# Sinkhorn attention and a bilinear feed-forward on one core: a gate on batch 0's second halves, and q of two more head pairs transposed by DMA

## Chip, core and metric

The kernel runs on one core of one Trainium2 chip. The metric is the time of one execution on the device in microseconds, as a median of several runs; lower is better. TensorE is called PE in the profile (its weight loads PEld), VectorE DVE, ScalarE ACT, GpSimd POOL, SyncE SP.

## What is computed

Four batches, eight heads, 768 tokens, 64 values a head. The sequence is cut into 8 blocks of 96. A small 8 by 8 matrix for each head is normalised five times over rows and columns and mixes the blocks of k and v; attention then runs inside each block. The heads are put side by side (512 values a token) and go through a feed-forward of two projections, their product, and an output projection.

```python
for _ in range(5):
    P = P - max(P, -1); P = exp(P)
    P = P / (sum(P, -1) + 1e-9); P = P / (sum(P, -2) + 1e-9)
k_s = einsum('bhij,bhjcd->bhicd', P, k_blocks)   # the same for v
attn = softmax(q_blocks @ k_s.T / 8)             # 96 x 96 in each block
x = (attn @ v_s) as (4 * 768, 512)
out = ((x @ w_a) * (x @ w_b)) @ w_out            # w_a, w_b 512 x 1536, w_out 1536 x 512
```

Inputs and output are fp32; the kernel's matmuls take bf16, which the loads make of the inputs.

## The kernel before

Heads are worked two at a time: a batch has four pairs, and 128 partitions hold two heads of 64. For a pair the steps are:

- q is transposed (`q_part`): twelve TensorE transposes (`q_pe`, L555) into a PSUM bank and a copy out by ACT or DVE into qT. Where `QDMA(b, p)` holds, which it does for batch 3, there is one DMA transpose on SP instead (`q_dma`, L707), and q is loaded by two DMAs with 64 values to a piece (`q_wide`, L434) instead of one (L483).
- k and v are mixed (`mix_half`, L582, for batch 0; `mix_part`, L571, for the others), and copied out to kT and vT.
- v is brought to tokens by TensorE transposes (`v_pe`, L641), or from the seventh pair on by one mix in token order (L619) and a trip through DRAM on SP (L628 out, L632 back).
- scores (L660), exponential on ACT (L665), output (L675), reciprocal and product on DVE (L681, L686).
- x is transposed: for batch 0 by TensorE (`x_part`, L694) and a copy, for the others by one DMA transpose a pair on SP (L702).

Batch 0 is worked in two halves of four blocks each, h = 0 and h = 1, so that the feed-forward of the first half of its tokens can begin early. Its two projections are plain matmuls (`ab_plain`, L836). Batches 1 to 3 use seven products in place of eight (`ab_strassen`, L930); sums of weights and of x that these need run on DVE or POOL (L373). The output projection is `out_plain` (L987), its results go to DRAM from SP (L1007). Until 32.6 us of the plan, gaps of TensorE are filled with matmuls on zeros (`warm`, L1222).

All loads are issued by POOL, in order. `load` lets about 2.8 MB of loads be on their way at a time.

Nothing is scheduled by hand line by line. Each step is a piece of work (`add`) with its engine or a choice of engines, an estimated time, what it depends on, and the buffers and PSUM banks that it takes and gives back. `Plan.solve` goes through the pieces in an order and gives each an engine and a place; the instructions are emitted by the starts that come out. The order is written out: the string ORDER holds for each piece its number and which of its engines it takes. Dependencies of the plan that carry no data, such as the gate of the second halves, shape the plan and so the order that was written out; on the chip an engine waits for data and buffers.

The gate before the change, for batch 0's second halves (L1169 to L1175):

```python
R0 = 10.0
for p in range(HP):
    st["gate", p] = st["last", p]
for p in range(HP):
    rk = R0 + 5.0 * p
    go = st["gate", p]
    qd = q_part(0, p, 1, rk, go)
```

`st["last", p]` is the last piece of pair p's first half (the DVE product of L686).

Of the kernel before, what the change touches and what calls it, by code (L numbers as in the profile page):

```python
# [36 lines left out]
class Plan:  # L37
# [13 lines left out]
    def add(self, eng, dur, fn, deps=(), get=(), put=(), rank=0.0, lat=None, port=()):  # L51

        alts = dict(eng) if isinstance(eng, (list, tuple)) else {eng: dur}
        op = Op(alts, fn, deps, list(get), list(put), rank, lat, len(self.ops), port)
        for key in op.put:
            self.holders[key] = self.holders.get(key, 0) + 1
        self.ops.append(op)
        return op
# [171 lines left out]

RATE = 365e3
ORDER = (
    b"%z1C$e###%#'#)#+#/#-#1#5$g$i#7#;$k$m#A$o#=$q$s#G#3$u$w#C#M$y%^${#I$}#9#S%`%#%%#Y%'#O#?%)%+"
    b"#`#E%-%/#U#f%1%~%3#[#K%5#l&$%7%9#b#r%;#Q%=#W%?#x%A#h%C&@%E#n#^%G&B%I%K#t%M#d#~%O%Q%S#j$(#z"
    b"%U$.&_#p%W&a%Y$4%b%f#v%d$:%[$$&&%h&H)/&(%j&K%n%l&D&*#|%p&G&2$*&L&-&c$@&4$0%r&O&.)+$6%t&e&P"
    b"&1&g$<$&%v&R&o$B$,&j')&q$2'%$F',&T$8''&k&V'-$L$>&X&m&6&}$H)-'0&Z'#'f&8%x&^'^'h&:'b%|'j$D'a"
    b"&<'d$R$N&s'm'C&>&u'?-j'E&w'n'A'G(($J'p'J($$T'O(+$X'K(&'1'N'Q&y-r'|&|(,'3$P(#*0(/$Z*<$_*@-l"
    b"*>$V$a*2*D*B(>*8*4*F(D$]'S(@*6(J-_*H(P(F*:*T(V$c*J(L-Z(](B*V-c*P(c(R'U*L-e*](i(H*m'W(X-f*N"
    b"(N*X(_*R(T*o(o(e(0-i*u*a(u(Z-](k*Z(2({-a(a,8)%*_(q(4,:*c-v(g(6'Y(w*i(8*e(m+f'](}-p*g+i(s(:"
    b")''5*k(<*q(y)1+n'7*s'9)3)7+q)#'r)=*w';+r'=))-n-1+t't+j'v,4+l)9'x,<,7-t'z+v,>,]-3--)5,`+x,D"  # L240
    b")C,@-0,F-x*})?,C*y+z*{)I);+|+~+))O+%,H)E++)U,J,L,N)[)K+1+#)b)A+-,P+')Q)h,$)G+/,&)n)W+A+3)M"
    b")t,()^+C,*)S)z,e,,+I+5)d,g)Y*$+9)j+7,i)`**.Z+=)p,k,R.^+;)f,T+Y,V)v)l.c+?+M)|)r+[.e+O+b*&.g"
    b"+E)x,m+U/1*,.i+G/3)~,a+K,o-5,c*(+^-7+Q*..k,{-9,q,}+S.m+`,s+W-;._,.,00.+d.a/Y0*00,X/].y,2.o"
    b"0-.{,u.P,w.q-=,y,Z-?-#-A-%/^-'-C.(1E-)/`/5-+-K/7/--M.*/0/9.s.,/b.u/A.w../;-z/C/d/f.0/=/K-O"
    b"/M.}/h-Q-|/#/?.R/%-~02.T-E.$04.<-G-I06/j.&-S.V0>.>080@/E.A/O/l-U.2/G/Q.X/I.B/S-W/x0H0:/z/n"
    b".F.D/p0<0J1H/r/|/t1r/~/v.H1t.41I1v0$.J1L1z.6.L1x1M1|0B25.81~1O0D.N2$0F1U2&1Q.:1W2*2(1[1S26"
    b"202,1^221l1Y2.1`1b282:1h0L2<1j1d1n0N2>0P2B1f0V2D0X0]2@2_0c2H0_2a1q2F2Y2J2g0e0i2N0Z2c2i0o2L"
    b"2e0u0a2m2T0k2[2P2o2V0{2k0q2R2q1%0g4P0w2s4T2]2y3'0m4V2{3#2u3)0s3+4R2}2w3/1+3-4X313K0}0y4Z33"
    b"5#3M3%351'3S114]3F371-3O5%173U3;1#391=3Y3Q3A1)3=3[3C3G3W3?4e4_3j3^1/4g3`5O133z3I6L3f3h3l19"
    b"4a5Q4F151?1;3b6$4c/'0&3d4o6&3|3o5W4q/)5'5Y4H0(5)5S1A4#5[4<4J5|/+5U4L5^5d5~5+5f6(4$5-4(6*4N"  # L250
    b"5/5`4&6,4i/U4*514k574m4,5n5b4>0R594s6.4A425p/W4u534w4B0T646044664.5h55475r3p6N4D485j5t6S5l"
    b"625v6{405;6Q6}3r4:5=7#5?3t7'7%3v687)6V6T7+6:6X7>7-3x6<6_7/6Z6a73716e6]7?79756g7;6u6c776i6k"
    b"7A7C6q6>7E6s6w6m7G6@6o7K7I6y6B7M7h6D7O7c7j7Q6F7p7S7l7r7W7U7v7n7d7^7Y7x7`8*7t7[7z7|5A7f8&80"
    b"5C8(8,7~82848$5E88868.8T8:5G8<8O8V8>5I8]8@8X8_8D8B8c8Z8P8J8F8e8L8s8a8H8y8i8R8v9O8k9;4y5K8m"
    b"8x4{5M8g9'5x8o9Y4}8q6H5z8{9)8}9E6J9,9#9[9-919%9^9`9/9b9d939f9G969Q9I9l979T9h9n:u9U9j9=99:w"
    b"9r:'9K9?9p9W9t:y9A:}9x9M9v;#:{:(9z9~;'9C;79|;%;):$:*:,;-;+:.:0;:;3:4:2;/:6;5:J:8;1::;<;=:<"
    b";A;?:@:>;C:L;E:F:B;[:H;G;I:D;K:O:P;M:T:R;Q;O:V;^:X;W;S;Y:Z:o:];U:_;a;b:a;f;d:e:c;h:q;j:k:g"
    b":m;l<$;n:i;p:t<4;r;v<';t<H;|;~;x<R;z<)<J<T<L<6<W<><N<8<:<P<]<X<<<@<_<Z<B<*<b<D<c<,<F<.<0<e"
    b"<2"
)  # L260
STRASSEN_OUT = ()
QDMA = lambda b, p: b >= 3
VDMA = lambda b, p: 4 * b + p >= 6


@with_exitstack
def kernel(
# [259 lines left out]
    s_ok = {}  # L527
# [77 lines left out]
    def mix_copy(eng, b, p, what, h, tc_order):
        mix, to = buf((what + "m", b, p)), buf((what + "T", b, p))
        i0, n = (0, NB) if h is None else (h * NBH, NBH)
        o0 = 0 if h is None else h * HK
        if tc_order:
            copy(ENG[eng], _ap(to, o0, [[2 * HK, P], [1, n * BLK]]),  # L610
                 _ap(mix, i0 * CG, [[1024, P], [1, n * CG], [P, NCH]]))
        else:
            copy(ENG[eng], _ap(to, o0, [[2 * HK, P], [CG, NCH], [BLK, n], [1, CG]]),
                 _ap(mix, i0 * CG, [[1024, P], [P, NCH], [CG, n], [1, CG]]))
# [86 lines left out]
    def x_dma(b, p):  # L701
        nc.sync.dma_start_transpose(  # L702
            out=_ap(buf(("xT", b)), p * S, [[KA * S, P], [BLK, NB], [1, BLK]]),
            in_=buf(("xp", b, p)).rearrange("q i e d -> q (i e d)"))

    def q_dma(b, p):
        nc.sync.dma_start_transpose(  # L707
# [56 lines left out]
    def v_part(b, p, h, vsrc, rk):  # L764

        pe = add("PE", 0.28 if h is not None else 0.5, lambda: v_pe(b, p, h), [vsrc, o_ident],
                 get=[("bank", ("vp", b, p, h))], put=[("vT", b, p)], rank=rk)
        alts = (("ACT", 0.6), ("DVE", 0.42)) if h is not None else (("ACT", 1.0), ("DVE", 0.69))
        op = add(alts, None, None, [pe, o_pads, first.get(("v", b, p))],
                 get=[("vs", ("vs", b, p))] if h in (0, None) else [],  # L770
                 put=[("vp", b, p, h)], rank=rk)
        first["v", b, p] = op
        op.fn = lambda: v_copy(op.eng, b, p, h)
        return op
# [386 lines left out]
    for p in range(HP):  # L1161
        rk = float(p)
        qd = q_part(0, p, 0, rk)
        kd = mix_half(0, p, "k", 0, rk)
        vd = v_part(0, p, 0, mix_half(0, p, "v", 0, rk + 0.05), rk + 0.1)
        m = so_part(0, p, 0, True, kd, qd, vd, rk + 0.1)
        x_part(0, p, 0, m, rk + 0.15)
        st["last", p] = m
    R0 = 10.0  # L1169
    for p in range(HP):  # L1170
        st["gate", p] = st["last", p]
    for p in range(HP):
        rk = R0 + 5.0 * p
        go = st["gate", p]
        qd = q_part(0, p, 1, rk, go)  # L1175
        kd = mix_half(0, p, "k", 1, rk, go)
        vd = v_part(0, p, 1, mix_half(0, p, "v", 1, rk, go), rk + 1.0)
        m = so_part(0, p, 1, True, kd, qd, vd, rk + 1.0)
        x_part(0, p, 1, m, rk + 2.0)
    for p in range(HP):  # L1180
        load_pair(1, p, -2)
    later_spreads(5)
# [128 lines left out]
```

## Time and profile before

| what | value |
|---|---|
| median of 4 runs | 244.28 us (243.34 to 246.06) |
| the profiled execution | 243.34 us, span 241.6 us |
| granted TensorE clock, mean over the span | 0.998 |
| TensorE busy | 231.9 us, 96% of the span |
| DVE, ACT, POOL busy | 152.4, 115.3, 110.3 us |
| chain that ended last | TensorE 92%; L930 34%, L987 26%, L836 13% |
| first L836, first L987 in the chain | 29.91, 76.59 us |
| DMA | 27.88 MB, mean 115 GB/s |

The span runs from the program's first to its last instruction in the profile; the execution's time has 1.7 us around it. The chain is followed back from the last instruction: at each step to the work that released it, or to the instruction before it on its engine. A step called "issue" is time in which the engine waited for nothing that the profile shows.

### The profile page before, as it was taken

The page shows a single profiled execution, that of the slowest core. Times are in us where ns is not written, and L with a number is a line of the kernel's source. Part 1 is how long each engine was busy: PE and PEld are TensorE (multiplying, and loading weights), DVE is VectorE, ACT ScalarE, POOL GpSimd, SP SyncE. Part 2 cuts the span into 40 slices and gives each one's busy share as a digit, 9 for nine tenths or more (in the row PEclk, how much of TensorE's full clock was granted, in tenths as well). Part 3 has the DMA queues.
Part 4 walks back from the last instruction along what each step waited for, and adds up shares of the span by engine and source line. Part 5 has one row for each costly group of instructions (what it writes and reads, how often), then busy time and mean ns, then how long its engine had stood idle before and what let it go on. Part 6 is the DMA issues. An engine that isn't in the chain of part 4 may idle for free.

```text
span 241.6 us, 5480 instructions
## 1 busy us (share of the span) xinstructions
PE 231.9 (96%) x2196; PEld 132.5 (55%) x2196; DVE 152.4 (63%) x305; ACT 115.3 (48%) x174; POOL 110.3 (46%) x123
## 2 busy tenths in 40 slices
PE   8799799999999999999999999999999999999992
PEld 3367565675656555665554555655654455555440
DVE  6758637785746564678873565887663468877410
ACT  3367624485257443656572633666620166564110
POOL 8779999998300000559995004265240005433000
PEclk9999999999999999999999999999999999999999
DMA  5999999999976769319999699200143461000066
GB/s 68 181 200 159 200 170 176 174 188 198 201 167 141 66 152 204 82 42 98 145 197 116 139 200 226 59 3 1 19 49 65 87 138 39 0 0 3 0 130 130
DMA packets 50104, 27.88 MB, mean 115 GB/s; under 512 B 28832, under 2 KB 47008, under 8 KB 50080
## 3 DMA queue, kind: packets, MB, share of 16 engines
q0 software_dynamic: 24112, 14.16, 43.3%
q1 hardware_dynamic: 25968, 13.38, 28.6%
q8 instruction: 17, 0.28, 0.5%
q14 instruction: 7, 0.06, 0.1%
HBM read 30.29 MB, written 8.26 MB: 160 GB/s over the span
## 4 chain that ended last, share of the span: by engine, by line
PE 92%; DMA 2%; POOL 2%; ACT 1%; issue 1%; DVE 0%; ACTq 0%
PE ps L930 34%; PE ps L987 26%; PE ps L836 13%; PE ps L675 4%; PE ps L660 3%; PE ps L571 2%; DMA q<-in_q_dram 2%; PE ps L582 2%; PE ps L555 2%; PE ps L641 1%; PE ps L619 1%; PE ps L1222 1%; PE ps L694 1%; ACT kT L316 1%; POOL k L439 1%
## 5 line engine op out<-in xcount | busy, mean ns | idle before, releaser
L987 PE MATMUL ps<-w_out_sb,hT 128*128 128x512 bf16 x288 | 67.0, 379 | 0.0
L373 DVE TENSOR_TENSOR f<-f,ps 128x768 f32<-128x768 f32 x54 | 49.8, 951 | 22.3 <-PE ps L930 12.2
L373 POOL TENSOR_TENSOR hT<-f 128x384 bf16<-128x384 f32 x35 | 34.4, 1000 | 50.2 <-DVE f L373 50.1
L936 ACT COPY f<-ps 128x768 f32<-128x768 f32 x54 | 42.2, 800 | 29.8 <-PE ps L930 29.5
L987 PEld LDWEIGHTS <-hT 128*128 128x128 bf16 x288 | 26.8, 98 | 29.4
L665 ACT ACTIVATE eT<-ps 96x768 bf16<-96x768 f32 x32 | 24.9, 811 | 17.3 <-PE ps L660 15.5
L373 DVE TENSOR_TENSOR hT<-a,ps 128x384 bf16<-128x384 bf16 x42 | 22.0, 550 | 15.0 <-PE ps L836 11.0
L930 PE MATMUL ps<-tx,ws_a 128*128 128x384 bf16 x108 | 26.4, 326 | 0.1
L930 PE MATMUL ps<-tx,ws_b 128*128 128x384 bf16 x108 | 26.4, 326 | 0.0
L686 DVE TENSOR_TENSOR xp<-ps,rec 96x512 bf16<-96x512 f32 x32 | 21.6, 683 | 0.7
L930 PEld LDWEIGHTS <-ws_b 128*128 128x128 bf16 x144 | 14.1, 98 | 9.3
L930 PEld LDWEIGHTS <-ws_a 128*128 128x128 bf16 x144 | 13.6, 98 | 9.9 <-ACT f L936 0.5
L836 PE MATMUL ps<-xT,w_b_sb 128*128 128x384 bf16 x96 | 18.8, 326 | 0.0
L373 POOL TENSOR_TENSOR tx<-xT 128x768 bf16<-128x768 bf16 x2 | 3.3, 1631 | 34.0 <-DMA out_dram<-o 34.0
L847 ACT CAST a<-ps 128x768 bf16<-128x768 f32 x12 | 9.3, 800 | 19.0 <-PE ps L836 19.0
L836 PE MATMUL ps<-xT,w_a_sb 128*128 128x384 bf16 x96 | 18.2, 326 | 0.0
L966 ACT CAST a<-ps 128x384 bf16<-128x384 f32 x18 | 8.6, 478 | 18.9 <-PE ps L930 18.9
L930 PE MATMUL ps<-xT,w_a_sb 128*128 128x384 bf16 x72 | 17.6, 326 | 0.0
L930 PE MATMUL ps<-xT,w_b_sb 128*128 128x384 bf16 x72 | 17.6, 326 | 0.0
L316 ACT COPY o<-ps 128x512 f32<-128x512 f32 x15 | 8.6, 589 | 17.0 <-PE ps L987 16.8
L316 ACT CAST kT<-ps 128x768 bf16<-128x768 f32 (+1 forms) x19 | 12.9, 683 | 7.3 <-PE ps L571 6.6
L318 DVE COPY o<-ps 128x512 f32<-128x512 f32 x9 | 6.2, 690 | 14.2 <-PE ps L987 13.8
(95 smaller groups left out, 328.4 us busy)
## 6 DMA issues: line engine op xcount, KB each, us to landing
out_dram<-o SPq DMA_DIRECT2D x48, 128.0 KB, 2.4
k<-in_k_dram POOLq DMA_DIRECT2D x16, 192.0 KB, 6.1
v<-in_v_dram POOLq DMA_DIRECT2D x16, 192.0 KB, 6.3
vd<-vm SPq DMA_DIRECT2D x10, 192.0 KB, 3.1
vs<-vd SPq DMA_DIRECT2D x10, 192.0 KB, 3.2
q<-in_q_dram POOLq DMA_DIRECT2D x16, 96.0 KB, 5.1
w_a_sb<-in_moe_w_a_dram POOLq DMA_DIRECT2D x4, 384.0 KB, 6.1
w_b_sb<-in_moe_w_b_dram POOLq DMA_DIRECT2D x4, 384.0 KB, 6.0
```

The lines of the kernel that those rows point to most:

```text
L316: nc.scalar.copy(out=out, in_=in_)
L373: ENG[eng].tensor_tensor(out=out, in0=in0, in1=in1, op=op)
L660: nc.tensor.matmul(sc[:, e, i * BLK:(i + 1) * BLK], lhsT=kT[e * D:(e + 1) * D, at:at + P], rhs=rhs, start=True, stop=True)
L665: nc.scalar.activation(out=buf(("eT", b, p, h))[:, :, 0:HB], in_=buf(("sc", b, p, h))[0:BLK, :, 0:HB], func=AF.Exp, scale=float(scale))
L675: nc.tensor.matmul(ops_[:, e, i * OW:(i + 1) * OW], lhsT=eT[:, e, i * BLK:i * BLK + P], rhs=vs[:, h * NBH + i, e * OW:(e + 1) * OW], start ...
L686: nc.vector.tensor_tensor(out=_ap(xp, h * NBH * 2 * D, [[NB * 2 * D, BLK], [D, 2], [2 * D, NBH], [1, D]]), in0=_ap(ops_, 2, [[1024, BLK], ...
L836: nc.tensor.matmul(pf[:, u, 0:HW], lhsT=w_sb[:, kc, (m + u) * P:(m + u + 1) * P], rhs=buf(("xT", b))[:, kc, t * HW:(t + 1) * HW], start=(k ...
L847: ea = add("ACT", 0.8, lambda: nc.scalar.copy(out=buf(("a", b, t, m)), in_=buf(("pf", b, t, m, "a"))[:, :, 0:HW]), [ps_["a", 1]], get=[("a ...
L930: nc.tensor.matmul(buf(key)[:, n, 0:HW], lhsT=lf(n, j), rhs=rf(j), start=start and j == 0, stop=j == 1, skip_group_check=not start)
L936: return add("ACT", 0.8, lambda: nc.scalar.copy(out=buf((name, b, g)), in_=buf(kA)[:, :, 0:HW]), [dep], get=[("f", (name, b, g))], rank=rk)
L966: e21 = add("ACT", 0.48, lambda: nc.scalar.copy(out=buf(("c21", b, g))[:, 0, :], in_=buf(kA)[:, 0, 0:HW]), [p4], get=[("a", ("c21", b, g)) ...
L987: nc.tensor.matmul(po, lhsT=hT[:, t * 2 + m // G, m % G, c * P:(c + 1) * P], rhs=w_out_sb[:, m, :], start=(m == 0), stop=(m == KO - 1), sk ...
```

## The change

The gate of every pair's second half becomes the last piece of the last pair's first half. `QDMA` also holds for pairs 2 and 3 of batch 2, so their q is loaded by two DMAs each and transposed by SP. ORDER is another string, written for the plan with these pieces. Three new functions or switches come with it: `mix_first`, which with WHOLE false returns the old `mix_half`; XDMA, which is false for all pairs, so that x of batch 0 goes on by `x_part`; and `x_half_dma`, which is then not called. The limit in `load` is as it was. New lines move the line numbers behind them by up to 33 in the changed kernel.

```diff
 ORDER = (
-    b"%z1C$e###%#'#)#+#/#-#1#5$g$i#7#;$k$m#A$o#=$q$s#G#3$u$w#C#M$y%^${#I$}#9#S%`%#%%#Y%'#O#?%)%+"
+    b"1C$e%z###%#'#)#+#/#-#1#5$g$i#7#;$k$m#A$o#=$q$s#G#3$u$w#C#M$y%^${#I$}#9#S%`%#%%#Y%'#O#?%)%+"
 ...
 STRASSEN_OUT = ()
-QDMA = lambda b, p: b >= 3
+QDMA = lambda b, p: 4 * b + p >= 10
 VDMA = lambda b, p: 4 * b + p >= 6
+XDMA = lambda p: False
+WHOLE = lambda p, what: False
 ...
+    def mix_first(b, p, what, rk):
+
+        if not WHOLE(p, what):
+            return lambda h, r, after=None: mix_half(b, p, what, h, r, after)
 ...
+    def x_half_dma(b, p, h):
+        nc.sync.dma_start_transpose(
+            out=_ap(buf(("xT", b)), p * S + h * HB, [[KA * S, P], [BLK, NBH], [1, BLK]]),
+            in_=buf(("xp", b, p))[:, h * NBH:(h + 1) * NBH].rearrange("q i e d -> q (i e d)"))
 ...
     for p in range(HP):
         rk = float(p)
         qd = q_part(0, p, 0, rk)
-        kd = mix_half(0, p, "k", 0, rk)
-        vd = v_part(0, p, 0, mix_half(0, p, "v", 0, rk + 0.05), rk + 0.1)
+        km = mix_first(0, p, "k", rk)
+        kd = km(0, rk)
+        vm = mix_first(0, p, "v", rk + 0.05)
+        vd = v_part(0, p, 0, vm(0, rk + 0.05), rk + 0.1)
+        st["mix", p] = km, vm
 ...
     R0 = 10.0
     for p in range(HP):
-        st["gate", p] = st["last", p]
+        st["gate", p] = st["last", HP - 1]
     for p in range(HP):
         rk = R0 + 5.0 * p
         go = st["gate", p]
         qd = q_part(0, p, 1, rk, go)
-        kd = mix_half(0, p, "k", 1, rk, go)
-        vd = v_part(0, p, 1, mix_half(0, p, "v", 1, rk, go), rk + 1.0)
+        kd = st["mix", p][0](1, rk, go)
+        vd = v_part(0, p, 1, st["mix", p][1](1, rk, go), rk + 1.0)
         m = so_part(0, p, 1, True, kd, qd, vd, rk + 1.0)
-        x_part(0, p, 1, m, rk + 2.0)
+        if XDMA(p):
+            d = sp_dma(1.3, 0.65, lambda p=p: x_half_dma(0, p, 1), [m, x_home(0)],
+                       put=[("xp", 0, p)], rank=rk + 2.0)
+            xT_done.setdefault((0, 1), []).append(d)
+        else:
+            x_part(0, p, 1, m, rk + 2.0)
```

In the built program TensorE's list has 21 matmuls fewer (24 transposes of q fewer, three warm matmuls more), SP's has two DMA transposes more, and POOL's two load issues more. The two lists agree up to TensorE's first 186 instructions, and then order the same pieces differently: the changed one runs the first halves of all four pairs before the second halves.

More of the change, by code (lines that the diff above doesn't have):

```diff
@@ L232 @@
 ORDER = (
-    b"%z1C$e###%#'#)#+#/#-#1#5$g$i#7#;$k$m#A$o#=$q$s#G#3$u$w#C#M$y%^${#I$}#9#S%`%#%%#Y%'#O#?%)%+"
+    b"1C$e%z###%#'#)#+#/#-#1#5$g$i#7#;$k$m#A$o#=$q$s#G#3$u$w#C#M$y%^${#I$}#9#S%`%#%%#Y%'#O#?%)%+"
     b"#`#E%-%/#U#f%1%~%3#[#K%5#l&$%7%9#b#r%;#Q%=#W%?#x%A#h%C&@%E#n#^%G&B%I%K#t%M#d#~%O%Q%S#j$(#z"
-    b"%U$.&_#p%W&a%Y$4%b%f#v%d$:%[$$&&%h&H)/&(%j&K%n%l&D&*#|%p&G&2$*&L&-&c$@&4$0%r&O&.)+$6%t&e&P"
-    b"&1&g$<$&%v&R&o$B$,&j')&q$2'%$F',&T$8''&k&V'-$L$>&X&m&6&}$H)-'0&Z'#'f&8%x&^'^'h&:'b%|'j$D'a"
@@ L237 @@
[L237 to L254, printed above, removed]
@@ L255 @@
-    b"8x4{5M8g9'5x8o9Y4}8q6H5z8{9)8}9E6J9,9#9[9-919%9^9`9/9b9d939f9G969Q9I9l979T9h9n:u9U9j9=99:w"
-    b"9r:'9K9?9p9W9t:y9A:}9x9M9v;#:{:(9z9~;'9C;79|;%;):$:*:,;-;+:.:0;:;3:4:2;/:6;5:J:8;1::;<;=:<"
+    b"%U$.&_#p%W&a%Y$4%f%b#v%h$:%e$$&*%j%[&,%n&g%m)+%p&D&j&c#|&H&F&f%r$*&k&J%t&o$0%v&m&L$@$6&&&q"
+    b"&O%x)/$<&P$&&)&.%|$B$,&s&1&R$2&u&2&w$8&T&4$F$>&}&V&X$L$H'?'#&6'B(()-'%&8(*&:'G'b''$D(,'J'd"
+    b"$N'1(/'C$R'3'K'F')'f-j'N'+'O$J'i&y'-'Q$T&<&|'j&?&Z'/$X'S'm'^&]'U'5-l'W$P'|'`$Z($'7'~*<'9(&"
+    b"*0$_'n$V(>'Y*>'p$a'](D';*D'r'>*2(J't'v$]*4(P*8(@-_'x(V*H'{(F-Z*L(]$c-]*X(c(L-g*6(B(i-a*Z(R"
@@ new lines @@
+    b"*:-v*J(H(X*N*P(N*T(o-c(_*m*R(u(T*V(e({*o-e(Z*])%(k-i(0*u+f(a)1*_,4(q(2-r*q(g+i(w(4,7*s(m(6"
+    b",a)7(8(}+j,c*w)=(s(:,])')C+l+n(=(y*@,`)I)3+q,q)#)O+v,s+r-t*B))+x+u+Y*F)9,$)U+[,&-x--+b+))5"
+    b"-0+z+++|)[)?+~+E+1-p-5+M-7);+A)b-9+-)E-n+C-;+/+I+G)K)A+3)h*})Q)G)n+O+K*y+U)W,(*{)M)t,*-=)^"
+    b",,,e+%+#)S,g-?)z*a+')Y,i,8*$)d-1,:,k*c)`**-3._)j*e*i-A)p)f*g.a+5*k-C)v,{)l+7,},m,<+=)r+9,>"
+    b",o.c+;.e)|,@)x/1+?.g,B*&/Y-K.2.i/3*,)~-M/[,D*(.4,F/^.k.7,N/`,H.8+^,J,P,L+Q.m*.+`0*+S+d.:,R"
+    b",.,0.Z+W/b0,.].(/d,2,T/f,V.y.o/h,X.{.*02.,-E04.P.q..,Z-G-I06/j-O.0/n-Q.R-S/p08,u.F1F.U-U/l"
@@ new lines @@
+    b",w,y.V-W/x.H/z.s0:.K-#/-.X-%.L.<.u/00<.w-'.N/K-)/5/M/A/7.>/C/r-z.A/9-+/t.B/v/;.}0./#/|/%.D"
+    b"00-|1J/~1M/=0$-~0H1O.$1Q/?1H0>0J1S1U0@1r.&1L1W0B1Y0D1t0F1[1m/E1^1z/G/I1`1|1b/O1h2$/Q1n1j1d"
+    b"2&/S1v1f0L2(0N1p2_1x202a0P1~24222c0V2*2g0X0]2e2,2i0c0_2m2.2k2o0e0i2~3'0Z290o2q2s3)0u0a4T2y"
+    b"273/0k4V2{2u0{0q3$314X1%3+2w0g4P0w351+3-0m2:374Z330s2<3E4R393;4]3%5'3A2B5)3C3G0}0y3=2D5#2>"
+    b"113?1'4_2H172@5+3I2J3K5%1#5-2F2X3M2L1)5/2N1=4a4e1-2T3S2[4g2P2V513U4o2R3O4q4c3Y3Q2]5W3[5713"
+    b"5Y3j1/3W53595O3^193`55423f6L5[3m3h151?5Q3b1;6$/'/U3d4i6&4<4k3o/)5^1A0R44/W3z465|/+5`4s4(48"
@@ new lines @@
+    b"0T4u4m4w5~0&6N5S6(5U4*5b6*3|4,5n4:4#5d6,5p4F4.0(5f4$6.405r4H5t646Q4J5h4&4>605j663p5l4L4@62"
+    b"5v4B6R4N6T805;82845=4D5?3r88863t6V8:3v8O688<6X6:6<8>6_3x8@6Z6a8D8B6e6]8P8J8F6g8L6u6c8H6i6k"
+    b"6>8R6q7h6@6s6w6m7j6B6o7l7p7n6y6{7r6D7t8+6}7v6F7'7x7#7)7|7z7-7%8,8&7~7/8(7=7+8$71735A8.797C"
+    b"5C7;7?757E5E777G7K7I7A8T7M5G7O7c8V7Q5I8]7S8X8_7W7U8c8Z7d7^7Y8e7`8s8a7[9'8i7f8v8k9O4y4{8m8x"
+    b"5K4}9E6H5M5x8y6J5z9G919I9K9Q8g9S9M9;8o9Y9[9U8q9a939W9d9^959)9b9f979h9,9=9j9l9-9?8{999n:u:'"
+    b"9A8}9r9/:w9p9#:y9t9C:}9x9v;#:{9%:(9z9~;'9|;7;%;):$:*:,;-;+:.:0;:;3:4:2;/:6;5:J:8;1::;<;=:<"
@@ L257 @@
     b";A;?:@:>;C:L;E:F:B;[:H;G;I:D;K:O:P;M:T:R;Q;O:V;^:X;W;S;Y:Z:o:];U:_;a;b:a;f;d:e:c;h:q;j:k:g"
-    b":m;l<$;n:i;p:t<4;r;v<';t<H;|;~;x<R;z<)<J<T<L<6<W<><N<8<:<P<]<X<<<@<_<Z<B<*<b<D<c<,<F<.<0<e"
-    b"<2"
+    b":m;l<$;n:i<4:t;p<*;r;v<';t;x;|<>;~;z<)<6<@<8<,<C<]<:<.<D<<<H<0<F<_<J<2<a<R<M<c<N<T<e<V<X<P"
+    b"<Z"
 )
 STRASSEN_OUT = ()
-QDMA = lambda b, p: b >= 3
+QDMA = lambda b, p: 4 * b + p >= 10
 VDMA = lambda b, p: 4 * b + p >= 6
+XDMA = lambda p: False
+WHOLE = lambda p, what: False
 @with_exitstack
@@ L603, in mix_half, with part @@
         return op
+    def mix_first(b, p, what, rk):
+        if not WHOLE(p, what):
+            return lambda h, r, after=None: mix_half(b, p, what, h, r, after)
+        pe = add("PE", 0.46, lambda: mix_pe(b, p, what),
+                 [(k_in if what == "k" else v_in)[b, p], s_ok[b, p]],
+                 get=[("pair", (what + "m", b, p))], put=[(what + "2", b, p)], rank=rk)
+        def part(h, r, after=None):
+            op = add((("ACT", 0.48), ("DVE", 0.56)), None, None,
+                     [pe, o_pads, first.get((what + "T", b, p))],
+                     get=[(what + "T", (what + "T", b, p))] if h == 0 else [],
+                     put=[(what + "m", b, p)], rank=r)
+            first[what + "T", b, p] = op
+            op.fn = lambda: mix_copy(op.eng, b, p, what, h, False)
+            return op
+        return part
     def mix_copy(eng, b, p, what, h, tc_order):
```

## The prediction

> **What bounds the kernel now.** I read the page's first and fourth parts, then a table of busy time by stage, then the chain of waits around the one hole that the table shows.
>
> ```profile
> span 241.6 us, 5480 instructions
> PE 231.9 (96%) x2196; PEld 132.5 (55%) x2196; DVE 152.4 (63%) x305; ACT 115.3 (48%) x174; POOL 110.3 (46%) x123
> PE 92%; DMA 2%; POOL 2%; ACT 1%; issue 1%; DVE 0%; ACTq 0%
> ```
>
> TensorE is busy 96% of the span and carries 92% of the chain that ended last. No other engine is near it. So an edit counts by the TensorE work that it adds or removes, and by the waits of TensorE that it makes or ends.
>
> ```profile
> 24.00:30.00 6.00, 4.25 (x124) 3.43 (x122) 3.52 (x9) 4.11 (x8) 5.96 (x6) 1.00 1.30 200
> 30.00:36.00 6.00, 6.00 (x45) 3.70 (x44) 2.36 (x6) 1.50 (x2) 5.98 (x8) 1.00 1.20 171
> 36.00:75.00 39.00, 38.96 (x485) 24.80 (x484) 26.69 (x55) 20.22 (x28) 25.15 (x28) 1.00 1.12 181
> 75.00:100.00 25.00, 24.85 (x292) 13.45 (x287) 14.30 (x30) 12.26 (x18) 2.04 (x2) 1.00 0.72 130
> 100.00:150.00 50.00, 49.87 (x398) 27.48 (x397) 33.69 (x52) 25.70 (x38) 27.14 (x31) 1.00 0.99 140
> 150.00:236.98 86.98, 86.90 (x518) 47.27 (x516) 55.05 (x79) 38.39 (x57) 23.93 (x24) 1.00 0.24 48
> ```
>
> The first number after the stretch is its length, the second TensorE's busy time. From 30 us to the last matmul TensorE lacks 0.04 + 0.15 + 0.13 + 0.08 = 0.4 us in all. Waits that a better order could remove are worth 0.4 us there, no more. The hole is before 30: the six microseconds from 24 hold 4.25 of matmuls. The chain names it:
>
> ```profile
> 27.67 0.22 PE ps L641 x2
> 27.89 1.75 issue
> 29.64 0.27 PE ps L641 x2
> ```
>
> Two matmuls of one set of four L641 transposes run, TensorE stands 1.75 us, then the other two run. All four read the same tile, so no data, buffer or gate can be what is missing between them. What is missing is the instructions:
>
> ```profile
> q8 instruction: 17, 0.28, 0.5%
> ```
>
> 17 packets of 0.28 / 17 = 16.5 KB make up an instruction queue. TensorE has 2 x 2196 = 4392 matmuls and weight loads, some 258 to a packet. A packet of this queue moved at 16.5, at 21.2, at 27.2 and at 32.0 us. TensorE has a first such hole of 0.34 us at 18.55 us, again inside a set (L660). Both resume about 2.4 us after a packet began. In the built program's list of TensorE instructions the two holes lie 502 rows apart, about two packets. My reading is that the stretch from 17 to 30 us, where TensorE's matmuls are short, is paced by this queue behind the loads (DMA share over 1.2), not by the attention's order.
>
> On this there is a rule. The Trainium skill, page "Runtime: NRT & Kernel Launch", section "Instruction fetch mechanics", says that the sequencer refills in blocks of 256 instructions and that a crossing's cost is mostly hidden. The trace agrees with the block (258 a packet) and not with the hiding (1.75 us). By the rule the hole would not come back and the time would be about 1.8 us lower than my sum; I go by the row.
>
> **The change, part by part.** Two parts of its name move nothing: x of batch 0 stays on TensorE (XDMA is false, as the only path was before), the limit of 2.8 MB in `load` is the same line in both, and `mix_first` with WHOLE false returns the old `mix_half`. What moves is the gate, q of batch 2's pairs 2 and 3, and the written-out ORDER.
>
> *The gate and the order before 30 us.* Up to the twelve q transposes of pair 3 and one warm matmul TensorE's list is the same. Then all first halves run, with three more warm matmuls between them, and second halves follow. In the old list L836, the first product of the feed-forward, begins at row 946, in the new at row 968. The hole sits at row 942. There the new list has the middle of a mix of second half (L582, k of pair 3). If the same packet arrives at the same time, TensorE reaches L836 at 29.64 + 12 x 0.026 = 30.0 us, against 29.9. So whatever the gate does before row 942 costs and wins nothing: the packet hides it. The bounds are a hole gone (-1.75) and one as much longer as the two known holes differ (1.75 - 0.34 = +1.4). I take 0, since loads, their order and the code size up to there are the same.
>
> *TensorE's work behind row 942.* Counted from both lists, with the chain's own pieces as prices (L555 x12 0.46, L675 x8 0.26, L660 x8 0.28, L582 x12 0.31, L641 x8 0.55):
>
> - 24 L555 fewer (the two q transposes): 2 x 0.46 = -0.92
> - 16 L675 fewer (done earlier): -0.52
> - 8 L660 and 12 L582 more: +0.28 + 0.31
> - 1 L641 fewer: -0.07
>
> That is -0.92. The new list changes from one line to another 162 times behind that row, the old 148 times. In the timeline a set of twelve L571 or L555 matmuls starts one each 0.028 us, 0.34 in all, and its piece is 0.46, so a change of shape can cost 0.12; most changes (L987, L836, L930 to L675) cost nothing in the chain's pieces. 14 more changes are worth 0 to 14 x 0.12 = 1.7; I take +0.4, three or four of the dear ones. Sum of the work: -0.5.
>
> *q of two pairs by DMA.* Removed besides: two DVE copies of 0.55 us, off the path (DVE 63%). Added and moved:
>
> ```profile
> L483 POOL DMA_DIRECT2D q<-in_q_dram x8 | 5.8, 731 | 0.0
> L434 POOL DMA_DIRECT2D q<-in_q_dram x8 | 6.6, 836 | 0.0
> L707 SPq DMA_TRANSPOSE qT<-q x4: 1210/1212/1240, 115.8 to 136.1; - x4
> DMA to landing us min/median/max: 2.7/4.9/7.1
> 82.61 0.46 PE ps L555 x12
> ```
>
> On POOL two issues of 0.73 become four of 0.84, +1.9 us; POOL is 46% busy. On SP come two transposes of 1.21. SP is in order: before the first one stand five issues of the v round trip (L628, L632), behind it the vs reload of the next pair and the first stores. When must the result be there? L836 starts at 30.0, and to the first L987 stand 176 L836 (28.6), 64 L660 (2.2), 32 L675 (1.0), 96 L571 (3.7), 48 L555 (1.8), 16 L694 (1.1), 16 L641 (1.1) and 6 L619 (1.0), 40.5 us: L987 starts near 70.5 (old: 76.6). Then 34 L987 (7.3), 16 L836 (2.6) and some 3.7 us of attention stand before the first scores on such a q: 84.1 us. The loads stand at the same places of POOL's list as the old ones, issued at 59.5 and 62.3. With the longest landing of q's rows (8.3) and a second issue they are there at 69 and 72. A transpose at its longest landing (7.1) ends at 76 to 79. Cover: 5 us at least; without it each microsecond late is one of TensorE. I take 0.
>
> The Trainium skill, page "VectorE: DVE Perf Modes", section "The three transpose paths", speaks against this edit: a 128 by 128 transpose is 390 ns on TensorE and 1309 ns by DMA. Six tiles a pair would by that be an estimated 2.3 against 7.9 us, and two pairs 11 us slower if they stood on the path. The trace has 0.46 against 4.9 us and the 4.9 covered.
>
> *Later stages.* The new order puts four sums of x of batch 1 on POOL (1.63 each) where two were, and batch 3's loads behind three products of 1.0. Batch 3's first k is issued after the last output of batch 2 on DVE. Between that output's matmuls and the first mix of batch 3 stand 40 L930, 6.5 us. Against that: DVE 0.2 + 0.68 behind one sum of 0.95, about 1 us of POOL's queue, and the shortest landing of k, 3.4: 6.2. Cover 0.3 us; I take 0. Its bounds are 0 and, with the longest landing of k (8.1), +4.4. The waits of 0.4 us that the old list had may stay or go: -0.4 to 0.
>
> **Sum.** The profiled execution took 243.34 us, 241.6 of span and 1.7 around it. -0.5 gives 242.8. The runs' median is 244.28, 0.94 above the profiled one, so the median becomes 243.8, 0.2% less. Differences under 1% (2.4 us) are about what a measurement of this kernel can't tell from none.
>
> **Rivals.** *The hole goes.* The packet for row 942 moves earlier, or TensorE has it in time. For it: the first hole was only 0.34 us, so luck decides. Against: loads run at 200 GB/s there in either version. It gives -0.5 - 1.75 - 0.4 = 241.6.
>
> *Batch 3's loads come late.* The place is the first mix of k of batch 3, near 113 us. The point from which it decides is a landing above 3.7 us. At 3.7 more, a little under the longest landing, it costs +3.7: 244.28 - 0.5 + 3.7 = 247.5, slower. For it: k's median landing is 6.1. Against: in the slice before those loads (103 to 109 us) the DMA engines move 42 GB/s against about 200 in the loaded slices, and the 3.4 was measured there.
>
> *The q transposes block SP.* A vs reload behind them comes late. It needs over 5 us beyond the longest landing; one pair's worth late would give 244.28 - 0.5 + 1.5 = 245.3, still within 1%.
>
> **How the numbers follow.** Forecast, with the small q price in it, 0.56 (own range 242.6 to 245.3); hole gone 0.19; loads late 0.21; the rest 0.04. The range must reach both outer cases, so 241.4 to 247.2. Faster by over 1% is the hole's case and a little luck, 0.20; slower is the late loads and surprises of a rewritten order, 0.25; within 1% 0.55.
>
> **What would show it.** Right: L555 set counts down by 24; an "issue" hole inside a set near row 942, L836 starting within 0.5 us of 30; L987 near 70.5; TensorE without holes from there to the last matmul near 236.5. Wrong: no hole (then I am too high), or a TensorE wait on the k mix near 113 us or on SP's transposes near 84 us (then too low).

## The result, and the profile after

The changed kernel takes 245.74 us in the median of 38 runs, the kernel before 245.2 in 59 runs beside it: a ratio of 1.0024 with a 95% interval of 1.0003 to 1.0045, or +0.6 us (0.1 to 1.1). The forecast was -0.2%, or -0.5 us: the sign was wrong, and the two lie about 1.1 us apart. All ratios here are of the runs within 1.5% of their kernel's fastest; the slower ones are left out.

The profiled run of the changed kernel took 247.26 us, with this page:

```profile
span 245.5 us, 5440 instructions
PE 233.6 (95%) x2175; PEld 132.4 (54%) x2175; DVE 151.9 (62%) x304; ACT 116.2 (47%) x174; POOL 111.9 (46%) x124
PE 91%; DMA 2%; issue 2%; POOL 2%; ACT 1%; DVE 0%; ACTq 0%
```

TensorE is the bound as before. The span is 3.9 us longer than that of the profile before, much more than the medians say; where it lies is seen in the table by stage (length, then the busy time of PE, PEld, DVE, ACT, POOL, then the granted clock, the DMA share and GB/s):

```profile
24.00:30.00 6.00, 3.26 (x92) 2.60 (x89) 3.03 (x7) 2.64 (x6) 5.04 (x5) 0.90 1.16 174
30.00:36.00 6.00, 5.78 (x94) 4.52 (x93) 2.98 (x8) 3.63 (x7) 6.00 (x8) 0.81 1.09 148
36.00:75.00 39.00, 38.99 (x436) 24.03 (x435) 25.00 (x49) 19.79 (x27) 26.63 (x30) 1.00 1.26 188
75.00:100.00 25.00, 25.00 (x262) 13.24 (x261) 14.22 (x28) 9.61 (x13) 2.97 (x2) 1.00 0.70 145
100.00:150.00 50.00, 49.70 (x431) 27.28 (x427) 34.95 (x55) 27.46 (x40) 27.20 (x30) 1.00 0.94 130
150.00:241.00 91.00, 91.00 (x555) 49.32 (x550) 55.56 (x80) 41.22 (x62) 24.34 (x24) 1.00 0.25 52
```

Nearly all of it is ahead of 36 us. The six microseconds from 24 hold 3.26 of matmuls in place of 4.25, and the clock, 1.00 before, is 0.90 and 0.81. The chain of waits there (start, length, what):

```profile
23.55 0.88 PE ps L584 x42
24.43 2.74 issue
27.17 0.28 PE ps L584 x6
...
33.18 0.22 issue
33.40 0.38 PE ps L584 x12
33.78 0.27 PE ps L861
```

The hole is again inside one piece of work (L584, 42 matmuls and 6), and it is one block of instructions earlier than in the profile before: at matmul 345 of TensorE's list, not 470. It is followed by a slow spell. In slices of 1 us (length, busy PE, granted clock, DMA share, GB/s):

```profile
28.00:29.00 1.00, 1.00 (x38) 0.92 0.94 136
29.00:30.00 1.00, 1.00 (x26) 0.50 1.18 180
30.00:31.00 1.00, 1.00 (x14) 0.50 0.89 134
31.00:32.00 1.00, 1.00 (x16) 0.50 0.91 137
32.00:33.00 1.00, 1.00 (x35) 0.87 1.24 154
```

The lost clock is 0.08 + 3 x 0.50 + 0.13 = 1.7 us. So the first L861 starts at 33.8 us in place of 29.9. From there to the end of the last matmul the changed kernel needs 207.3 us, the kernel before 207.1: the forecast had this part 0.5 us shorter, and it did not get shorter, but the 3.9 us are not in it either.

### The profile page after: what moved, and what is told of

Read it like the earlier page. It is cut to its first block, busy times and chain, and to the rows that moved or that the text cites. A ratio compares the mean times of both kernels' runs of the same rounds, so it can differ in the third digit from the quotient of the medians.

```text
span 245.5 us, 5440 instructions
## 1 busy us (share of the span) xinstructions
PE 233.6 (95%) x2175; PEld 132.4 (54%) x2175; DVE 151.9 (62%) x304; ACT 116.2 (47%) x174; POOL 111.9 (46%) x124
## 4 chain that ended last, share of the span: by engine, by line
PE 91%; DMA 2%; issue 2%; POOL 2%; ACT 1%; DVE 0%; ACTq 0%
PE ps L955 34%; PE ps L1012 26%; PE ps L861 13%; PE ps L695 4%; PE ps L680 3%; PE ps L573 2%; DMA q<-in_q_dram 2%; PE ps L584 2%; PE ps L557 2%; PE ps L639 1%; PE ps L661 1%; PE ps L1255 1%; PE ps L714 1%; POOL k L441 1%; POOL v L441 1%
## 5 line engine op out<-in xcount | busy, mean ns | idle before, releaser
L375 DVE TENSOR_TENSOR f<-f,ps 128x768 f32<-128x768 f32 x54 | 50.4, 950 | 18.1 <-ACT f L961 10.1
L375 POOL TENSOR_TENSOR hT<-f 128x384 bf16<-128x384 f32 x33 | 32.6, 1003 | 53.0 <-DVE f L375 47.7
L685 ACT ACTIVATE eT<-ps 96x768 bf16<-96x768 f32 x32 | 25.4, 808 | 14.7 <-PE ps L680 14.3
L318 ACT COPY o<-ps 128x512 f32<-128x512 f32 x16 | 9.4, 584 | 29.0 <-PE ps L1012 29.0
L375 POOL TENSOR_TENSOR tx<-xT 128x768 bf16<-128x768 bf16 x3 | 4.9, 1633 | 34.7 <-DMA xT<-xp 21.3
L318 ACT CAST kT<-ps 128x768 bf16<-128x768 f32 (+1 forms) x16 | 11.3, 722 | 15.9 <-PE ps L573 13.1
L861 PE MATMUL ps<-xT,w_a_sb 128*128 128x384 bf16 x96 | 18.6, 326 | 0.0
L955 PEld LDWEIGHTS <-ws_a 128*128 128x128 bf16 x144 | 12.7, 97 | 10.3 <-DVE f L375 1.4
L861 PE MATMUL ps<-xT,w_b_sb 128*128 128x384 bf16 x96 | 18.3, 326 | 0.0
L955 PE MATMUL ps<-xT,w_b_sb 128*128 128x384 bf16 x72 | 17.6, 326 | 0.0
L701 DVE RECIPROCAL rec<-ps 96x8 f32<-96x8 f32 x32 | 6.3, 199 | 14.4 <-PE ps L695 13.9
L955 PEld LDWEIGHTS <-w_b_sb 128*128 128x128 bf16 x108 | 10.6, 98 | 7.0
```

The costliest lines, as they stand in the source:

```text
L318: nc.scalar.copy(out=out, in_=in_)
L375: ENG[eng].tensor_tensor(out=out, in0=in0, in1=in1, op=op)
L685: nc.scalar.activation(out=buf(("eT", b, p, h))[:, :, 0:HB], in_=buf(("sc", b, p, h))[0:BLK, :, 0:HB], func=AF.Exp, scale=float(scale))
L701: nc.vector.reciprocal(out=buf(("rec", b, p, h)), in_=_ap(buf(("op", b, p, h)), 0, [[1024, BLK], [512 + D, 2], [OW, NBH]]))
L861: nc.tensor.matmul(pf[:, u, 0:HW], lhsT=w_sb[:, kc, (m + u) * P:(m + u + 1) * P], rhs=buf(("xT", b))[:, kc, t * HW:(t + 1) * HW], start=(k ...
L955: nc.tensor.matmul(buf(key)[:, n, 0:HW], lhsT=lf(n, j), rhs=rf(j), start=start and j == 0, stop=j == 1, skip_group_check=not start)
```

## The experiments

I call the stretch up to the first feed-forward product (L836, in the changed kernel L861) the front and the stretch from it to the last matmul the rear. All ratios are to the kernel before, run beside the kernel on the same chip.

### Both kernels once more

No edit. Are the front's 3.9 us the change, or the one run?

> The kernel before, unchanged, for a second profile and for the granted clock of its timed runs. Front theory: what sets the two kernels apart lies ahead of the first feed-forward product (L836), where TensorE waits for blocks of its own instructions; a hole of about 2.7 us is followed by 3.4 us at half the granted clock, one of 1.75 us is not. Then this profile has the stretch from the first L836 to the last matmul at 207.1 us within 0.3, a first L836 anywhere from 29 to 34 us, and a spell of half clock only if one hole is over 2 us; and more of its timed runs have a mean clock of 0.995 or more than the 13 of 32 of the changed kernel. Rear theory: the front is luck, the same for both, and the changed kernel loses behind L836. Then the share of runs with a clock of 0.995 or more is near 13 of 32 here too, and their spans are about 0.6 us below the changed kernel's 242.1 to 243.1.

Measured: 0.9988 (0.9954 to 1.0021). The same program now has its first L836 at 31.9 us and a hole at matmul 345, with half clock behind it, although the hole is under the 2 us that the theory asked for:

```profile
24.30 0.27 PE ps L582 x9
24.57 1.68 issue
26.25 0.25 PE ps L582 x3
```

Its rear is 207.1 us, to 0.01 as before. Of its timed runs 3 of 12 have a mean clock of 0.995 or more.

> The changed kernel, unchanged, for a second profile. Front theory: first L861 to last matmul 207.3 us within 0.3 again; its start at 30 to 34 us, by where the holes fall, and half clock for 3.4 us only where a hole is over 2 us. Rear theory: the stretch behind L861 differs from 207.3 by more than 0.5 us, and the start of L861 is near 30 us.

Measured: 1.0009 (0.9971 to 1.0046). First L861 at 31.2 us, holes of 0.54, 1.92 and 0.60 us at matmuls 219, 345 and 471, no half clock. But the rear is 208.9 us, 1.6 more than expected, and the table of TensorE's waits (total, times, longest) has a line that the other profile lacks:

```profile
PE ps L680 <- DMA qT<-q: 1.2, 2, 0.7
```

What follows: the front differs as much between two runs of one program (29.9 and 31.9; 33.8 and 31.2) as between the programs. The front theory is wrong in its first half: over all timed runs of the first comparison 14 of 39 of the changed kernel have a mean clock of 0.995 or more, against 3 of 12 here for the kernel before. And there is something in the rear: scores of batch 3 that wait for the DMA transposes of q.

### The two parts of the change alone

`order_only` has the new gate and order, with q of batch 2 as before; `q_only` the old gate and order with the two DMA transposes.

```diff
--- order_only: from the changed kernel
-QDMA = lambda b, p: 4 * b + p >= 10
+QDMA = lambda b, p: b >= 3
--- q_only: from the kernel before
-QDMA = lambda b, p: b >= 3
+QDMA = lambda b, p: 4 * b + p >= 10
-            e = list(op.alts)[order[done] % 2]
+            e = list(op.alts)[order[done] % 2 % len(op.alts)]
```

> The changed kernel's gate and written-out order, with q of batch 2's pairs 2 and 3 back on TensorE (24 L557 more, two SP transposes fewer). Front theory: the front is that of the changed kernel, the stretch behind L861 is 0.9 us longer (208.2 us), the ratio to the kernel before 1.005 to 1.008. Rear theory in the form that the transposes on SP cost more than they save: as fast as the kernel before or faster, 0.996 to 1.000, stretch behind L861 207.0 us or less.

Measured: 1.0055 (1.0020 to 1.0090), +1.35 us. First L861 at 30.2 us. The rear is 210.2 us; 1.7 of that are lost to half clock behind a hole of 2.4 us, and the 208.5 left are 1.4 more than in the kernel before.

> The kernel before with its own gate and order, and only q of batch 2's pairs 2 and 3 by DMA transposes, at the places of the order where TensorE had them (TensorE has 24 L555 fewer). Front theory: the front is that of the kernel before, the stretch from the first L836 to the last matmul 0.9 us shorter (206.2 us), ratio 0.995 to 0.998, no wait of TensorE on the transposed q. Rear theory: TensorE waits for transposes or for what stands behind them on SP, the stretch is 207 us or more, ratio 1.000 to 1.006.

Measured: 0.9963 (0.9921 to 1.0005), -0.9 us. The two measured differences have opposite signs, and their sum, +0.45, is near the whole change's +0.6. The new order loses, clear of its interval; that the transposes win in the old order is not clear of it. TensorE waits nowhere for a transposed q of batch 2, but its 24 matmuls fewer uncover another wait, 0.6 us near 79 us:

```profile
PE ps L660 <- ACT kT L316: 0.6, 1, 0.6
```

The rear is 208.5 us, of which 1.4 are lost to half clock: 207.1 in place of the 206.2 expected. So next to nothing of the -0.9 is seen in this profile's rear; the uncovered wait takes what the 24 matmuls give.

### Old front with new rear, and the reverse

Two written-out orders were joined at the first product: the pieces up to it from one, the rest in the other's sequence.

```diff
--- front_new: from the kernel before
-ORDER = (old)
+ORDER = (new up to the first ab_plain, then old)
-        st["gate", p] = st["last", p]
+        st["gate", p] = st["last", HP - 1]
-            if o.start > self.warm_until:
+            if o.start > 25.0:
--- rear_new: the same with the two exchanged and the old gate
```

> The new gate and the new order up to the first feed-forward product, the old order behind it, q of batch 2 as before; no filling matmuls behind the first product. Theory that the new order loses behind the first product: the stretch from the first product to the last matmul is that of the kernel before less what was moved ahead of it (206 to 207 us), ratio to the kernel before 0.998 to 1.002. Theory that the gate costs in the front: ratio 1.003 to 1.007, with the loss ahead of the first product in the profile, beyond the run's own holes.

Measured: 1.0131 (1.0098 to 1.0164). The rear is 208.8 us.

> The old gate and the old order up to the first feed-forward product, the new order behind it, q of batch 2 as before. Theory that the new order loses behind the first product, about 1.0 us by 16 more changes of matmul shape and a wait of 0.3 us near 113 us, less 0.4 us of work done earlier: ratio 1.002 to 1.006. Theory that the gate costs in the front: 0.998 to 1.001.

Measured: 1.0127 (1.0084 to 1.0169). The rear is 212.5 us, 1.6 of them lost to half clock. Both are slower than either whole order, which no theory had. The waits of front_new at the seam, between 44 and 49 us, say why: the order behind the seam expects other tiles to be ready.

```profile
PE ps L674 <- DVE hT L372: 0.7, 1, 0.7
PE ps L835 <- ACT a L846: 0.7, 1, 0.7
```

So the pair does not tell front from rear. One thing in it counts: rear_new waits 1.2 us for a transposed q of batch 3, as one profile of the changed kernel did, and front_new does not.

```profile
PE ps L659 <- DMA qT<-q: 1.2, 1, 1.2
```

### What a change of shape costs

In the traces a change of line on TensorE has the same price wherever it stands and no wait comes in: 0.09 us into L660, L571 or L555 (64 rows or 64 columns of the array) from a product that uses all of it, 0.11 to 0.12 us out of them, nothing for L675 behind a product. By these prices the rear's changes cost 6.9 us in the kernel before (65 that cost something), 7.9 in the changed one (75) and 8.1 in order_only (77). In the profile before, ten L987 take 0.1 us longer behind L660 than behind L675:

```profile
92.59 2.16 PE ps L987 x10
94.75 0.62 PE ps L660 x24
95.37 2.26 PE ps L987 x10
```

To test it, the scores of the kernel before are cut in two, with TensorE's next piece between the halves:

```diff
+def halve(order):
...
+        late = Op({"PE": 0.0}, lambda fn=op.fn: fn((2, 4)), [op], [], op.put, 0.0, None, -1)
...
+        op.fn, op.put = (lambda fn=op.fn: fn((0, 2))), []
+        order.insert(j + 1, late)
...
-    order = plan.solve()
+    order = halve(plan.solve())
```

> The kernel before, with 11 pieces of scores (L660, eight matmuls) cut in two: the last four go behind TensorE's next piece. The same matmuls, 169 changes of line behind the first feed-forward product in place of 147. Theory that the new order lost about 1 us by its changes of shape: a trip from whole-array products to scores and back costs 0.09 + 0.11 us beyond the matmuls wherever it stands, so by the prices of each pair of lines in the profile before the stretch from the first L836 to the last matmul grows by 3.0 to 3.5 us (210.1 to 210.6) and the ratio to the kernel before is 1.011 to 1.016. Rival, that changes are hidden in the flow of matmuls and the loss has another cause: under 0.5 us, ratio 0.998 to 1.003.

Measured: 1.0274 (1.0218 to 1.0331), more than expected. The rear is 212.8 us, +5.7: by the prices +2.9 for 28 more dear changes, the rest waits, 1.7 us of them of L675 for the exponential, since the second half of a piece now comes later. In the chain of split_scores:

```profile
93.78 2.16 PE ps L987 x10
...
97.47 2.16 PE ps L987 x10
99.63 0.53 PE ps L660 x20
100.17 2.27 PE ps L987 x10
102.43 0.21 PE ps L660 x4
```

Ten L987 take 2.16 us behind L675 and 2.27 behind L660. Twenty L660 take 0.53, four take 0.21: 0.02 each and some 0.1 to get in. The rival, that the flow hides it, is out. How much of the +5.7 is price and how much wait rests on the prices, not on the ratio.

### The batch 3 transposes

In the old order the first transposed q of batch 3 is there 3.1 to 3.8 us before its scores (landed at 123.0, used at 126.8 us in the profile before). In the new one it has 0.1 us (128.3, 128.3) in the first profile, 0.0 in the second, where TensorE waits, and 0.8 in order_only. The first scores of batch 3, before and after (count, ns, first and last start):

```profile
L660 PE MATMUL ps<-qT,kT x24: 202/203/213, 126.8 to 138.3; 64*128 64x96 bf16 x24
L680 PE MATMUL ps<-qT,kT x24: 202/203/213, 128.3 to 132.2; 64*128 64x96 bf16 x24
```

Counted from the first product, the changed kernel has these scores at 94.6 us in place of 96.9, and issues the first transpose at 86.2 in place of 85.9. So 2.3 us of the lost cover are the order's own; the transpose's length is the smaller part, 8.3 to 8.9 us with the new rear (after, after again, order_only, rear_new) against 7.1 and 7.7 in the two profiles of the kernel before. In the other kernels with the old rear it took 6.1 to 9.8 us and still landed 1.4 us or more ahead. For this test k and q of the third pair are loaded about 5 us later, out of the transposes' way:

```diff
+    third, fourth = sorted((loads[3, p] for p in range(HP)), key=lambda x: x[0].start)[2:]
+    for op in (third[0], third[2]):
+        order.remove(op)
+        order.insert(order.index(fourth[0]), op)
```

> The changed kernel, with k and q of batch 3's third pair loaded behind the next sums on POOL, some 3 us later. Theory that batch 3's transposes of q are late in the new order because they share the DMA engines with six loads: the first transpose lands in 7.5 us or less after its issue in place of 8.3 to 8.8, TensorE has 1 us or more in hand at the first scores of batch 3 and does not wait there; the changed kernel's time less 0.3 to 0.6 us, ratio to the kernel before 0.998 to 1.001. Rival, that the transpose's own length or SP's queue sets it: 8 us and more again, ratio 1.001 to 1.003.

Measured: 1.0104 (1.0061 to 1.0147). The transposes behave as the theory said; shortest, median and longest, in the window of batch 3:

```profile
DMA to landing us min/median/max: 2.8/4.6/5.9
```

The second profile of the changed kernel has this in the same window:

```profile
DMA to landing us min/median/max: 2.8/6.0/8.9
```

The first two now land 2.5 and 4.0 us ahead of their scores, and no score waits. The time got worse all the same: POOL's two sums of hT stand behind the moved loads, and TensorE waits 1.0 us for what DVE makes behind them (126.36 to 129.41 in the chain):

```profile
126.36 1.99 POOL hT L375 x2
128.35 0.02 issue
128.38 1.03 DVE hT L375 x2
129.41 0.05 issue
129.46 0.66 PE ps L959 x3
```

Another 1.2 us of this rear is half clock behind a hole of 2.3 us. That loads beside them stretch the transposes is what this one profile says (5.9 us against 8.3 to 8.9); that the wait can be had away for nothing is not shown.

### What paces the front

Three kernels on the ground of q_only.

```diff
--- q_few_warm
-            if cols >= 64:
+            if cols >= 64 and t > 7.0:
--- q_late_warm
-            if cols >= 64:
+            if cols >= 64 and t < 11.5:
--- q_fewer_loads, in load
+        near, n = nbytes, len(ld_n)
+        for k in reversed(range(n)):
+            near += ld_n[k][1]
+            if near > 1.6e6 and 12 <= n < 24:
+                behind = ld_i[k]
+                break
```

> The kernel before with q of two pairs of batch 2 by DMA, and without the 17 filling matmuls before 7 us of the plan, so that the first feed-forward product is TensorE's matmul 456 and not 473. Theory that TensorE is paced up to there by blocks of about 126 matmuls with their weight loads, at fixed numbers of its list: the holes stay at matmuls 219, 345 and 470, the first product begins ahead of the third and its long matmuls cover it; the first product starts 1 to 2.5 us earlier, ratio to the same kernel with all filling matmuls 0.990 to 0.996, so 0.986 to 0.992 to the kernel before. Rival, that the filling matmuls hold the clock up: a granted clock below 1 ahead of 17 us, and no gain or a loss of up to 2 us. Rival, that the holes belong to the work and not to the number: the holes stay in front of the same pieces of work, no change (0.996).

Measured: 1.0006 (0.9952 to 1.0060), from four of its twelve runs, of 243.5 to 246.2 us; the profiled execution took 248.8 us, and what follows is read from that one. The holes agree with the block theory, and the first product is late, as its first rival had it. The holes stay near matmuls 219 and 345 with 17 matmuls of work moved ahead of them, and there is none near 470, where L836 now runs. But the filling matmuls that are left run at half speed:

```profile
9.18 0.53 PE ps L555 x12
9.71 4.15 PE ps L1222 x10
13.87 0.46 PE ps L555 x9
14.32 1.25 PE ps L1222 x3
```

4.15 / 10 = 0.42 us each; in the profile before nine took 0.22 each at this place:

```profile
11.39 1.96 PE ps L1222 x9
```

The clock column reads 1.00 there, but the trace's clock records begin only with the first full clock: at 15.3 us here, at 5.1 in the profile before, where the fills ahead of it take 0.43 us each as well. So TensorE comes to full clock 10 us later here; a hole of 2.8 us with half clock behind it follows, and the first L836 begins at 35.2 us. By this profile the first fills are needed.

> The kernel before with q of two pairs of batch 2 by DMA, and without the 13 to 14 filling matmuls behind 11.5 us of the plan; the earlier ones stay. The first feed-forward product is TensorE's matmul 460. Theory that blocks of 126 matmuls pace TensorE up to there and that the long first products can cover a hole: no hole near matmul 470, the first product 1 to 2 us earlier than with all filling matmuls, ratio to the kernel before 0.988 to 0.994. Rival, that the filling matmuls are needed for TensorE's speed: a gap of about 2 us near 11.5 us and matmuls of twice the time or a spell of half clock behind it, ratio 0.996 to 1.005.

Measured: 0.9970 (0.9933 to 1.0008). The profile has half clock from 14 to 21 us and still its first L836 at 30.0 us:

```profile
14.00:17.00 3.00, 2.30 (x63) 2.11 (x64) 1.57 (x4) 1.71 (x4) 2.57 (x5) 0.50 1.29 190
17.00:21.00 4.00, 4.00 (x80) 3.05 (x77) 2.16 (x6) 2.58 (x4) 3.98 (x4) 0.53 1.28 194
...
24.00:30.00 6.00, 5.94 (x176) 4.88 (x170) 5.03 (x13) 5.39 (x11) 5.96 (x5) 1.00 1.25 175
```

0.50 x 3 + 0.47 x 4 = 3.4 us of clock are lost, with 13 matmuls fewer to do, and the first product is not later than with full speed: no hole is left. TensorE runs slowly where it would have stood for instructions. The missing hole is the theory's sign; the half clock and the ratio are the rival's. Against q_only (0.9963) nothing is won.

> The kernel before with q of two pairs of batch 2 by DMA, and loads 12 to 23 issued so that at most 1.6 MB of them are on their way, in place of 2.8. Theory that a block of instructions stands behind the loads in the DMA engines: from a block boundary to its packet 2.3 to 3 us in place of 2.3 to 5, the hole at matmul 345 under 0.5 us, no spell of half clock ahead of the first product, ratio to the kernel before 0.988 to 0.993. Rival, that the packet's delay has nothing to do with the loads on their way: delays up to 5 us as before, ratio 0.996; or the loads themselves come later, TensorE waits for q of the second halves or for w_a and w_b, ratio over 1.

Measured: 1.0202 (1.0162 to 1.0241). The holes go, as the block theory had it, and the time does not. From the start of matmul 219 or 345 to the next instruction packet the traces have, with 2.8 MB of loads on their way, 2.3 and 3.7 us (before), 4.0 and 2.5 (before again), 4.9 and 4.0 (after), 3.9 and 2.9 (after again), 1.7 and 4.8 (order_only); with 1.6 MB it has about 2.4 and 1.3. The 2.4 lies among the others, so one value of 1.3 is all that speaks for a packet that comes sooner. TensorE resumes from a hole 2.2 to 2.7 us after a packet, once 3.3 (front_new). No hole is left at these matmuls, but the loads are late:

```profile
PE ps L561 <- DMA q<-in_q_dram: 3.0, 4, 1.8
PE ps L842 <- DMA w_b_sb<-in_moe_w_b_dram: 1.3, 1, 1.3
```

and TensorE, idle in between, has half clock for 10 us. With TensorE late, a block has more time to come, so this run does not tell whether the loads delay the packets.

### A version with a lower time

q_late_warm, with three pieces brought beside like ones and an L675 put ahead of the two scores that wait for kT:

```diff
+                    if ok and far:
+                        late = max((d.end for d in o.deps), default=0.0)
+                        if late <= op.start + 0.3:
+                            del order[j]
+                            order.insert(i + 1, o)
...
+            nxt = next(o for o in pe[n + 2:] if kind.get(id(o)) != "scores_pe")
+            ahead(nxt, op)
-    order = plan.solve()
+    order = regroup(plan, plan.solve())
```

> The kernel before with q of two pairs of batch 2 by DMA, without the filling matmuls behind 11.5 us of the plan, with three pieces moved ahead so that alike pieces stand together (143 changes of line behind the first feed-forward product in place of 146), and with one output product (L675) ahead of the two scores that wait 0.56 us for kT near 78 us. Theory that TensorE's work, its changes of shape and its waits add up: the stretch from the first L836 to the last matmul 0.4 us less for the changes and 0.3 for the wait than the 206.97 us without these moves, 206.2 to 206.4; ratio to the kernel before 0.992 to 0.997. Rival, that the moved pieces wait for what their old places hid: 207 us or more, ratio 0.997 or more.

Measured: 0.9896 (0.9832 to 0.9960), 243.08 against 245.97 us: 1.0% below the kernel before, and the changed kernel is not below that one. Its profile does not confirm the reason: the rear is 207.4 us, as the rival said. The wait for kT became one for hT,

```profile
PE ps L675 <- DVE hT L373: 0.6, 1, 0.6
```

and two holes of 0.25 and 0.30 us took what the grouping gave. Its front is short (first L836 at 29.1 us). How much of the 1% belongs to the moved pieces stays open; the intervals of this kernel and q_late_warm overlap.

## Why the prediction was wrong, point by point

**The two DMA transposes: right in the new order.** I took -0.92 us. Order_only and the changed kernel differ in the rear by 0.67 us of L557 and 0.2 of its changes of shape. In the old order q_only's -0.9 (-1.9 to +0.1) would fit, but its rear shows at most 0.2 of it, for a reason that I did not have: the wait for kT. The cover was at least the 5 us that I named: in the changed kernel the transposed q of batch 2 is there 11.5 and 19.5 us before its scores. The tile's lines for batch 2 (issues, then landing):

```profile
L732 SPq DMA_TRANSPOSE qT<-q x2: 1258/1278/1297, 74.4 to 79.8; - x2
DMA to landing us min/median/max: 2.8/2.8/2.8
```

The first L987, for which I had 40.5 us behind the first product, came 40.8 behind it.

**The changes of shape: the step that failed first.** I counted 14 more changes, took "three or four of the dear ones" and wrote +0.4. In the rear there are 12 more dear ones from the order (65 against 77), at 0.09 to 0.12 each, +1.2 us; the q part takes two of them back, which leaves +1.0 in the changed kernel against my +0.4. The prices were in the profile and my mechanism was right; the size was off because I counted changes of line and not pairs of shapes. The Trainium skill, page "TensorEngine Tiling (Array Packing)", section "Key Properties", says that changing the tiling mode drains TensorE. I did not weigh it. The rows agree with it, at about 0.2 us for a trip there and back, if the 64-row and 64-column matmuls count as another mode, which no run here tells.

**Batch 3's loads: the right place, the wrong consumer, and the second step that failed.** I gave 0.3 us of cover to k at the first mix of batch 3. In the second profile k landed at 114.0 us and was used at 115.2, 1.2 us in hand. What had none was q, loaded behind k and v and then transposed. I did not follow that chain to its scores, which the new order has 2.3 us sooner behind the first product, and I had costed a transpose at 7.1 us at most where it took up to 8.9. So a wait that I put at nothing costs 0 to 1.2 us from run to run, 1.2 in two of the four profiles whose rear has the new order unaltered.

**The sum again.** In the rear, against the kernel before: matmuls -1.0 (24 L555, 16 L675 less, 8 L660 more), changes +1.0, together 0; the rear went from 207.1 to 207.3, so +0.2 is left over that no run assigns. With the wait for q in half of the runs, an estimate from those four profiles, the rear gives +0.8. Measured were +0.6 (0.1 to 1.1). So of the 1.1 us between forecast and result some 0.6 is the size of the changes and some 0.6 the wait for q. For the order alone -0.3 + 1.2 + 0.2 = 1.1, with the same wait 1.7, against 1.35 (0.5 to 2.2). My range ended at 247.2 us, below the 247.5 of my own case of late loads, which it was to reach.

**The hole: not refuted on average, wrong in its bounds.** I said that packets of instructions set the start of the first product and that the gate wins and costs nothing there. First products began at 29.9, 31.9, 31.9, 30.9 and 31.9 us with the old front (before, before again, q_only, rear_new, split_scores) and at 33.8, 31.2, 30.2, 30.8 and 32.3 with the new one (after, after again, order_only, after_loads_later, front_new), which does not tell them apart: a cost of the gate of some tenths of a us is not excluded. But my bounds, -1.75 to +1.4, came from two holes of one run. The hole can move to another block, and half clock can follow: 1.7 us that I did not have. It followed holes of 1.68 to 2.81 us in eight profiles, and not those of 1.75 and 1.92 us in the first of before and the second of after, so the hole's length alone does not decide it. The Trainium skill, page "TensorE: Matmul & The Clock Gate", section "What's actually happening", has half rate after an idle window of about 3.4 us; here a shorter gap was enough. The spells have the length that the page gives its window: 1.7 us lost at half rate are 3.4 us. The rule weighed in the prediction (page "Runtime: NRT & Kernel Launch", section "Instruction fetch mechanics"), that a crossing is mostly hidden, does not hold in this front: crossings cost 0.2 to 2.8 us, at least once in 12 of the 14 profiles.

**The base.** My 243.8 stood on a median of four runs, 244.28; with 59 runs the same kernel has 245.2, so the ratio, not the microseconds, judges the forecast.

## What to carry to other kernels

When TensorE is busy all the time, count its work by pairs of neighbouring shapes and price each pair from the trace, for a new order can lose in shape changes what it wins in matmuls. A hole in one profile is one draw: look at a second profile of the same program before a change is blamed or bounded by it. When a list is rewritten, check each chain of a later batch to its last link (load, transpose, first use), with durations under the load that the new order puts beside it.

## What was not expected of the hardware

- Where TensorE stood for a block of its instructions (126 matmuls with their weight loads), the block began 4.6 to 7.2 us after the one before it. From a packet to the end of the hole it was 2.2 to 2.7 us, once 3.3.
- Slow work in front of such a block was nearly free in one profile: with half clock for 6.8 us, and 13 filling matmuls fewer, the first product came at 30.0 us, as early as in the profile before.
- TensorE's first matmuls take twice their time until the first full clock, which came at 5.1 us in the profile before and, without matmuls ahead of 9 us, at 15.3. The profile's clock column reads 1.00 ahead of it, since its records begin only there.
